# A gated scan followed by a top-1 mixture of experts: another set of planner numbers, modality numbers built by groups of runs, weights loaded between the first inputs

## The chip, the core and the metric

The kernel runs on one core of one Trainium2 chip. The metric is the device time of one execution in microseconds (us): the median of the runs, 940.31 us for the kernel before (three runs, 939.61 to 948.43). One more execution was taken with the hardware profiler; every time of a row or a stretch below is of that execution.

Engines: PE is TensorE (matmuls), DVE is VectorE, ACT is ScalarE, POOL is GpSimd, SP is SyncE. SP only issues DMAs here; its queue works in order, so a DMA whose condition is open holds up all that stand behind it. Each of the other engines works through its own instructions in order too.

## What is computed

Four sequences of 5056 tokens with 256 channels pass through a gated linear recurrence; each resulting token (20224 rows of 256) then goes through one of eight experts. Biases that depend on a token's modality (0 or 1) are added to the router's logits.

```python
a_t = np.exp(8.0 * sig_r * np.log(a_base))          # per token and channel
x_gated = np.sqrt(np.maximum(1 - a_t * a_t, 1e-6)) * sig_i * x
h = a_t[:, t] * h + x_gated[:, t]                    # for t in range(5056): y[:, t] = h
...
logits = y @ w_gate + modality_bias[modality_id]     # 8 experts
e_idx = np.argmax(logits, axis=1)
out[mask] = gate_w[mask, None] * (np.maximum(y[mask] @ w1[e], 0) @ w2[e])   # mask: e_idx == e
```

## The kernel before

**Chunks.** The scan runs over 22 chunks of time (`STEPS`: 96, three times 128, 17 times 256, 224 steps of all four sequences). A chunk's three inputs `a`, `g`, `x` are loaded by SP (`load_chunk`), ACT makes tanh, exp, square and root, DVE gates and scans (`scan_chunk`, `gate_chunk`). `size_chunk` finds a power of two that brings the chunk into 16-bit floats; `split_chunk` and `low_parts` write the result as a high part (ACT) and a low part (DVE). PE makes the logits `psl` from them (L878). `route_chunk` adds the modality bias on DVE (L950, which needs `bm` and `ivl`, both from POOL), finds the expert of each token and its slot in a table `rows` in DRAM. `rows_part` turns the split chunk into rows (four DMA transposes `rt<-a` on SP) and scatters them with indirect DMAs from POOL (L1096).

**Pages.** Two experts take most tokens (`HOT = 2`). Their tokens are worked on in pages of 128, then 256, later 512 rows: DVE chooses a page's place in `rows` (`choose_two`, the tile `sel`), SP reads that number and loads the page transposed (`X<-rows`, L1354), PE computes layer 1 (`ph`, L1452) and layer 2 (`po`, L1498). The first two pages (`Xfirst`) are not read back from DRAM: PE picks their rows out of chunk 0 (`px`, L1049). A matmul in 32-bit accuracy is made of three 16-bit ones, so every weight is split too: `convert` makes a high half (`HI`: on ACT or DVE, one letter for each of two parts) and a low half in four pieces. For a weight with `D` in `LO` DVE makes the pieces (L444); with `P` PE does, by a 32-bit matmul with a diagonal and a 16-bit one with minus the identity (`pl`, L449 and L450), and ACT copies them out (L452). Weights 0 and 1 are the two layers of the first hot expert, 2 and 3 those of the second.

**Modality numbers.** `modality_order` is one thread on POOL: it brings the modality of every token into the layout of the chunks. Chunk by chunk size it copies the numbers (`mf`, L763 and L770) and makes their complement (`mg`, L775): first chunk 0 (3 columns), then chunks 1 to 3 (12 columns), then the 17 chunks of 256 steps (136 columns), then the last chunk (7 columns). `modality_bias` then makes a chunk's `bm` on POOL (L791, L796).

**What sets the order.** The program is laid out once by a planner in the kernel: threads ask for an engine with an estimated duration; of those that could start within `WINDOW` the planner takes the one with the least rank (`place`: a base, `C_STEP` per chunk, and hand-set numbers in `RANK`). The result is a fixed order for each engine. Where the planner sees PE idle for more than 0.5 us, `fill` (L331) puts matmuls on a constant there, 1.25 times as long as the gap that it expects. A scatter waits for the page matmul that the planner had placed last before it (`count["pe"]`), so a late PE delays scatters too.

Of the kernel before, what the change touches and what calls it, by code (L numbers as in the profile page):

```python
# [46 lines left out]
WINDOW = 0.09  # L47
# [3 lines left out]
HI = ["A", "AD", "A", "AD", "A", "D"]  # L51
LO = "DDPPDD"
START = "0 1 w w w w 2"
MODALITY = 14.11
PACED = 2
AHEAD = 7.0
LAND = 1.1
SHOW = 0.5
W_AT = 11.91
C_STEP = 2.31  # L60
GROW = 1.01
SIZE_LAG = 3.0
# [3 lines left out]
SLACK = 5.0  # L66
EARLY = 4
URGENT = 0.0
ROW_STEP = 2.4
LAG = 3.0  # L70
W_RANK = [10.2, 11.1, 7.0, -6.5]
W_LOW = [3.7, 5.6, -4.4, 2.1]
PICK_AT = 6.87
PICK = 14.12
# [3 lines left out]
    "load": [0.0, 2.1, -7.6, -1.3, 0.0, 3.0, 1.1, 10.3, -1.0],  # L78
    "scan": [-1.4, -9.0, -3.3, -2.8, -0.5, -0.3, -0.9, 2.7],
    "gate": [0.0, 0.0, 0.0, 3.3, 0.0, 0.8, -1.0, -4.7, 3.7, 0.3],  # L80
    "size": [1.7, 0.0, 0.0, 0.0, 1.4, 0.0, 0.0, 0.8],
    "split": [0.0, -1.5, 0.5, -4.1, 0.0, -0.5, 0.0, 0.4, 6.0, 3.6],
    "low": [9.8, 9.6, 0.0, -12.2, 0.0, -1.7],
    "route": [-6.4, 0.0, 0.0, 0.0, 0.6, -0.3, 2.3],
    "gates": [0.0, -2.2, 4.2, 5.5, 0.0, 0.0, 0.0, 0.0, -1.0],
    "rows": [0.0, 1.1, -0.6, 0.0, 0.0, 0.0, 0.9, -3.5, 0.0, 2.2],
# [35 lines left out]
def kernel(  # L122
# [156 lines left out]
    slots = {t: Slots(n) for t, n in BUFS.items()}  # L279
    free = {"PE": 0.0, "ACT": 5.7, "DVE": 5.9, "POOL": 9.0, "DMA": 2.1, "queue": 1.2}  # L280
# [18 lines left out]
    def give(tag, n):  # L299
        slots[tag].back[n] = plan["end"]  # L300
# [261 lines left out]
    def load_chunk(c):  # L562

        t0, T = CHUNKS[c]
        cols = 2 * B * T
        base = 2 * B * t0
        z = T / 256
        got = tiles[c] = []
        if f"{c}" in loads:
            yield "SP", 0.0, seen(("turn", loads.index(f"{c}") - 1)), 0.0  # L570
        else:
            yield "SP", 0.0, allof(drained(sum(B * t for _, t in CHUNKS[: c + 1]) - BACKLOG), seen(("load", c - 1))), -3.0
        n = max(1, T // P)
        for name, src in (("a", rs), ("g", gs), ("x", xs)):
            tag = "H" if c == 0 and name != "g" else name
            for i in range(n):
                yield "DMA", 2.9 * z / n, allof(room(tag) if i == 0 else seen(), paced(c)), -9.0
                if i == 0:
                    tickets[c, name] = tag, take(tag)
                    t = (pm if tag == "H" else pa).tile([P, cols], F32, name=f"{name}{c}", tag=tag, bufs=BUFS[tag])  # L580
                    got.append(t)
                w = cols // n
                ins = LOADS.dma_start(t[:, i * w : (i + 1) * w], src[:, base + i * w : base + (i + 1) * w])
                if c >= PACED:
                    tc.add_manual_dep(
                        ins.ins, pace[-2], mybir.DependencyInfo(mybir.DependencyClass.Sync, mybir.DependencyReason.DATA)
                    )
                pace.append(ins.ins.name)
                landed.append(plan["end"] + 0.1)
            mark["load", c, name] = plan["end"] + (SLACK if c >= LATE else 0.0)  # L590
        if c == 0:
            yield "DMA", 0.2, None, -9.0
            nc.sync.dma_start(wg, w_gate.rearrange("(h p) e -> p h e", p=P))
            yield "DMA", 0.2, None, -9.0
            nc.sync.dma_start(mb, mbias.rearrange("m e -> (m e)").partition_broadcast(P))
            yield "DMA", 0.5, None, -9.0
            nc.sync.dma_start(mid, modality.bitcast(I32).rearrange("p (c two) -> p c two", two=2))
        went(f"{c}")
        mark["load", c] = plan["end"]
        if c + 1 < NC:  # L600
            start_chunk(c + 1)
# [130 lines left out]
    def modality_order():  # L732

        yield "POOL", 0.4, room("X")
        tx = take("X")
        scratch = pm.tile([P, 5, COL[-1]], BF16, name="mq", tag="X", bufs=BUFS["X"])
        first, mq = scratch[:, 4], scratch[:, 0:4]
        nc.gpsimd.tensor_copy(first, mid[:, :, 0])
        for h in range(2):
            yield "PE", 0.2, room("ph")  # L740
            tp = take("ph")
            ps = psh.tile([P, 2, 256], F32, name=f"pm{h}", tag="ph")
            for a in range(2):
                nc.tensor.matmul(
                    ps[:, a, 0 : COL[-1]], sel4[:, 2 * h + a].rearrange("p g b -> p (g b)"), first, start=True, stop=True
                )
            yield "ACT", 0.35, None
            nc.scalar.activation(mq[:, 2 * h : 2 * h + 2], ps[:, :, 0 : COL[-1]], AF.Copy)
            give("ph", tp)
        c = 0  # L750
        while c < NC:
            T, n = CHUNKS[c][1], 1
            while c + n < NC and CHUNKS[c + n][1] == T:
                n += 1
            cs = slice(COL[c], COL[c + n])
            for g in range(B):
                yield "POOL", max(1, T // P) * (0.17 + 0.022 * n) * (1 if T % P == 0 else 2), None, 0.0
                gp = slice(Q * g, Q * g + Q)
                if T % P == 0:
                    src = mq[gp, :, cs].rearrange("p a (n g w) -> p n g w a", n=n, g=B)[:, :, g]  # L760
                    to = mf[gp, cs, 0].rearrange("p (n w a) -> p n w a", n=n, a=4)
                    for w in range(T // P):
                        nc.gpsimd.tensor_copy(to[:, :, w], src[:, :, w])  # L763
                    continue
                assert n == 1
                a, A = 0, T // Q
                while a < A:
                    q = g * A + a
                    k = min(A - a, 4 - q % 4)
                    nc.gpsimd.tensor_copy(  # L770
                        mf[gp, COL[c] + a : COL[c] + a + k, 0], mq[gp, q % 4 : q % 4 + k, COL[c] + q // 4]
                    )
                    a += k
            yield "POOL", 0.15 + n * 0.01, None, 0.0
            nc.gpsimd.tensor_scalar(  # L775
                out=mg[:, cs], in0=mf[:, cs], scalar1=-1.0, scalar2=1.0, op0=ALU.mult, op1=ALU.add
            )
            for i in range(c, c + n):
                mark["modality", i] = plan["end"]
            c += n  # L780
        give("X", tx)

    def modality_bias(c):

        C = columns(c)
        yield "POOL", 0.25 + 0.125 * C, seen(("modality", c))
        shc = [P, C, E]
        mc = slice(COL[c], COL[c + 1])
        bm = sm.tile([P, C, E], F32, name=f"bm{c}", tag="bm", bufs=3)
# [10 lines left out]
    def size_chunk(c):  # L800
# [36 lines left out]
        yield "POOL", 0.2, None  # L837
        nc.gpsimd.tensor_tensor(out=ivl, in0=iv, in1=ivg, op=ALU.mult)
        mark["ivl", c] = plan["end"] + 0.2

    def split_chunk(c):
# [8 lines left out]
        add(modality_bias(c), (0, place("low", c)), plan["end"])  # L850
# [7 lines left out]
    def low_parts(c, yg, ys, sc):  # L858
# [12 lines left out]
        yield "PE", 0.35 + 0.35 * z, room("lg"), 1.25 if c > 6 else 0.0  # L871
# [16 lines left out]
    def rows_part(c, j):  # L888
# [24 lines left out]
        yield "POOL", 0.2, lambda: at, 0.0  # L913
# [3 lines left out]
        yield "POOL", 0.2, seen(("gates", c)), 0.0  # L917
# [3 lines left out]
        nc.gpsimd.tensor_scalar(  # L921
# [10 lines left out]
    def route_chunk(c):  # L932
# [19 lines left out]
        )  # L952
        yield "DVE", small, None
# [27 lines left out]
        yield "DVE", small, seen(("counted", c - 1)) if c else None  # L981
# [25 lines left out]
        yield "POOL", 0.2, None  # L1007
        bh = sm.tile([1, HOT, E], F32, name=f"bh{c}", tag="bh")
        nc.gpsimd.tensor_tensor(
# [3 lines left out]
        yield "POOL", 0.5, None, 0.0  # L1013
# [142 lines left out]

    def routed(t=FAR):
        n = 0
        while n < NC and all(mark.get(k, FAR) <= t for k in [("b2", n)] + [("put", n, j) for j in range(parts(n))]):
            n += 1  # L1160
        return n

    def enough():
# [3 lines left out]
        for c in range(NC):  # L1167
            at = max([at, mark.get(("b2", c), FAR)] + [mark.get(("put", c, j), FAR) for j in range(parts(c))])
# [7 lines left out]
    def new_page(size, e, sel, col, late):  # L1176
        pg = Page()
        pg.size, pg.st, pg.e, pg.sel, pg.col, pg.routed, pg.late = size, size, e, sel, col, routed(plan["end"]), late
        return pg
# [18 lines left out]
    def choose_two(size, full):  # L1198

        sel, ticket = new_sel()  # L1200
        b2 = tiles["b2", routed(plan["end"]) - 1 if pages else 0]
# [21 lines left out]
        for e in range(HOT):  # L1223
            pg = new_page(size, e, sel, e, not full)
# [10 lines left out]
    def choose_cold(masked):  # L1235
# [32 lines left out]
        pg = new_page(P, None, sel, 0, True)  # L1268
# [58 lines left out]
    def load_rows(n=0):  # L1327
        while True:
# [5 lines left out]
            if True:  # L1334
# [3 lines left out]
                else:  # L1338
                    yield "DMA", 0.05 + st / 140, room("X"), 0.2, 1.65 if st <= 256 else 2.9
# [46 lines left out]
    def page_gates(t):  # L1386
        pg = t.pg
        yield "POOL", 0.25, lambda: max(t.known, mark.get(("hot", pg.e), FAR) if pg.e is not None else 0.0)
# [143 lines left out]
    def start_chunk(c):  # L1532
# [4 lines left out]
        add(size_chunk(c), (0, place("size", c)), urgent=early)  # L1537
        add(split_chunk(c), (0, place("split", c)), urgent=early)
# [92 lines left out]
```

## Time and profile before

| | us |
|---|---|
| median of three runs | 940.31 |
| profiled execution, whole | 936.71 |
| its span, first to last instruction | 935.0 |
| PE busy in the span | 920.6 (98%) |
| DVE, ACT, POOL busy | 630.4, 584.5, 509.3 |
| granted TensorE clock, mean | 1.000 of full speed |

The profiled execution is 3.60 us under the median. "Busy" counts a matmul from its start to the end of its result, and neighbours overlap; so what one matmul costs PE is read from the starts of two neighbours in the timeline, not from a row's mean duration. A wait in a row's brackets is the idle time of that engine just before it, and what ended it.

### The profile page before, as it was taken

To read this page: it belongs to the slowest core of one execution; us is meant where nothing else is said; L and a number is where in the kernel's file an instruction comes from. 1 tells how busy PE (TensorE), PEld (TensorE's weight loads), DVE (VectorE), ACT (ScalarE), POOL (GpSimd) and SP (SyncE) were. 2 spreads that over 40 slices of the span, in tenths; PEclk is the share of its full clock that TensorE was granted. 3 is DMA by queue.
4 is the path that set the end of the run, shared out by engine and by line. 5 is a ranking of instruction groups with operands and counts; after the bars stand their busy time and mean duration, and the time that the engine had idled before them with its cause. 6 is when DMAs were issued, how large, how long until landed. Compare 5 with 4: busy or idle time off the path is not lost. (4 is left out here: it accounts for less than half of the span.)

```text
span 935.0 us, 19535 instructions
## 1 busy us (share of the span) xinstructions
PE 920.6 (98%) x7222; PEld 657.9 (70%) x7222; DVE 630.4 (67%) x1434; ACT 584.5 (63%) x810; POOL 509.3 (54%) x731
## 2 busy tenths in 40 slices
PE   8999999999999999999999999999999999999997
PEld 4568777888887666666666666666666666666796
DVE  7998987887989777658777684688844233423521
ACT  8898788577768857567746766576543335333422
POOL 6766676866466556564654655566664425422222
PEclk9999999999999999999999999999999999999999
DMA  9779996898899677698398677586462335313110
GB/s 316 203 204 239 274 222 194 171 258 194 217 288 193 152 212 158 130 250 200 118 180 219 217 181 203 160 188 200 101 142 66 93 89 149 92 46 125 44 40 25
DMA packets 226938, 157.88 MB, mean 169 GB/s; under 512 B 195665, under 2 KB 200146, under 8 KB 226834
## 3 DMA queue, kind: packets, MB, share of 16 engines
q1 hardware_dynamic: 210562, 112.57, 51.6%
q0 software_dynamic: 16128, 43.98, 13.6%
q8 instruction: 58, 0.95, 0.4%
q14 instruction: 46, 0.38, 0.1%
q10 hardware_dynamic: 144, 0.00, 0.0%
HBM read 70.86 MB, written 44.48 MB: 123 GB/s over the span
## 5 line engine op out<-in xcount | busy, mean ns | idle before, releaser
L1452 PE MATMUL ph<-X,hw 128*128 128x512 f16 (+1 forms) x2400 | 452.8, 332 | 5.1 <-DMA X<-rows 5.1
L1452 PEld LDWEIGHTS <-hw 128*128 128x128 f16 x2496 | 237.0, 98 | 132.1 <-DMA X<-rows 6.8
L1498 PE MATMUL po<-hw,H 128*128 128x256 f16 x2448 | 298.4, 273 | 0.7 <-DVE H L1382 0.6
L1410 POOL DMA_INDIRECT out_dram<-ot,mt x160 | 182.0, 1137 | 183.0 <-ACT ot L1399 136.2
L1498 PEld LDWEIGHTS <-H 128*128 128x128 f16 x2496 | 241.9, 98 | 53.6 <-issue 1.6
L1096 POOL DMA_INDIRECT rows<-rt,di x158 | 181.4, 1148 | 170.4 <-PE ph L1452 79.4
L1382 DVE SCALAR_TENSOR_TENSOR H<-ph,H 128x512 f16<-128x512 f32 (+1 forms) x216 | 141.9, 665 | 130.0 <-ACT H L1380 129.3
L1380 ACT ACTIVATE H<-ph 128x512 f16<-128x512 f32 (+1 forms) x216 | 123.1, 578 | 134.3 <-PE ph L1452 128.4
L1498 PE MATMUL po<-hw,Hb 128*128 128x256 f16 x1344 | 165.1, 273 | 0.0
L1498 PEld LDWEIGHTS <-Hb 128*128 128x128 f16 x1344 | 130.6, 98 | 36.7 <-issue 0.8
L1382 DVE SCALAR_TENSOR_TENSOR Hb<-ph,Hb 128x512 f16<-128x512 f32 x112 | 76.6, 686 | 100.3 <-ACT Hb L1380 100.0
L1399 ACT ACTIVATE ot<-po,gt 128x256 f32<-128x256 f32 x160 | 75.4, 472 | 91.1 <-PE po L1498 78.2
L1380 ACT ACTIVATE Hb<-ph 128x512 f16<-128x512 f32 x112 | 66.4, 594 | 99.8 <-PE ph L1452 99.2
L669 DVE TENSOR_TENSOR_SCAN g<-a,g 128x512 f32<-128x512 f32 (+2 forms) x77 | 94.2, 1240 | 0.6
L652 DVE SCALAR_TENSOR_TENSOR g<-x,g 128x1024 f32<-128x1024 f32 (+2 forms) x39 | 48.1, 1233 | 24.4 <-ACT x L647 24.4
L865 DVE SCALAR_TENSOR_TENSOR a<-g,scy,a 128x512 f16<-128x512 f32 (+3 forms) x88 | 58.5, 695 | 4.9 <-ACT a L853 4.8
L853 ACT ACTIVATE a<-g,scy 128x512 f16<-128x512 f32 (+3 forms) x88 | 55.6, 672 | 2.7 <-DVE scy L700 2.0
L641 ACT ACTIVATE a<-a,ch 128x1024 f32<-128x1024 f32 (+3 forms) x44 | 49.6, 1148 | 0.0
L626 DVE SCALAR_TENSOR_TENSOR g<-g,x 128x1024 f32<-128x1024 f32 (+2 forms) x39 | 48.2, 1238 | 0.0
L807 DVE TENSOR_REDUCE top<-x 128x4 f32<-128x2048 f32 (+3 forms) x22 | 45.2, 2056 | 4.1 <-DMA x<-in_x_dram 4.1
L331 PE MATMUL fill<-onesb 128*128 128x512 bf16 x182 | 44.9, 396 | 1.1 <-DVE onesb L152 1.1
L647 ACT ACTIVATE x<-x,quarter 128x2048 f32<-128x2048 f32 (+3 forms) x22 | 40.2, 1828 | 0.3
(216 smaller groups left out, 675.5 us busy)
## 6 DMA issues: line engine op xcount, KB each, us to landing
a<-in_r_gate_dram SPq DMA_DIRECT2D x37, 512.0 KB
g<-in_i_gate_dram SPq DMA_DIRECT2D x37, 512.0 KB
x<-in_x_dram SPq DMA_DIRECT2D x37, 512.0 KB
wr<-in_moe_w_dram SPq DMA_DIRECT2D x4, 1024.0 KB
cw<-in_moe_w_dram SPq DMA_DIRECT2D x4, 1024.0 KB
out_dram<-ot,mt POOLq DMA_INDIRECT x160
rows<-rt,di POOLq DMA_INDIRECT x158
rt<-a SPq DMA_TRANSPOSE x88
```

Of the source, the lines that this page charges most:

```text
L626: nc.vector.scalar_tensor_tensor(out=g, in0=g, scalar=1.0, in1=x, op0=ALU.add, op1=ALU.mult)
L641: nc.scalar.activation(sl, sl, AF.Exp, scale=ch[:, h : h + 1], bias=ch[:, h : h + 1])
L669: nc.vector.tensor_tensor_scan(out=gi, data0=ai, data1=gi, initial=0.0, op0=ALU.mult, op1=ALU.add)
L853: nc.scalar.activation(ys[:, 0, :, g], yg[:, :, g, :].rearrange("p h (k b) -> p h k b", b=Q), AF.Copy, scale=sc[:, g : g + 1])
L865: nc.vector.scalar_tensor_tensor(out=ys[:, 1, :, g], in0=yg[:, :, g, :].rearrange("p h (k b) -> p h k b", b=Q), scalar=sc[:, g : g + 1], i ...
L1096: ins = nc.gpsimd.indirect_dma_start(out=rows[:, :], out_offset=bass.IndirectOffsetOnAxis(ap=idx, axis=0), in_=src, in_offset=None, bounds ...
L1380: nc.scalar.activation(hi, src, AF.Relu)
L1382: nc.vector.scalar_tensor_tensor(out=lo, in0=src, scalar=0.0, in1=hi, op0=ALU.max, op1=ALU.subtract)
L1399: nc.scalar.activation(t.ot[a // 2][:, a % 2, :], po, AF.Copy, scale=t.gt[:, a : a + 1])
L1410: ins = nc.gpsimd.indirect_dma_start(out=out[:, :], out_offset=bass.IndirectOffsetOnAxis(ap=t.mt[:, a, 0:1], axis=0), in_=t.ot[a // 2][:, ...
L1452: ins = nc.tensor.matmul(to, wv[:, s, k, f * P : (f + 1) * P], cur.X[:, 2 * x + k, :], start=(m == 0), stop=(m == len(mm) - 1))
L1498: ins = nc.tensor.matmul(po, H[:, hx, fi, a * P : (a + 1) * P], wv[:, wx, f], start=(f == 0 and m == 0), stop=(f == NF - 1 and m == 2))
```

## The change

The diff leaves what is computed as it is. Its core, without the estimates that only the planner reads (durations in `yield` lines):

```diff
-START = "0 1 w w w w 2"
+START = "0 w 1 w w 2 w"
-LO = "DDPPDD"
+LO = "PDPPDD"
-HI = ["A", "AD", "A", "AD", "A", "D"]
+HI = ["A", "AD", "DA", "A", "A", "D"]
-AHEAD = 7.0
+AHEAD = 6.41
+AHEAD_OF_ROWS = 1.04
+ON_DVE = 8
+BIAS_RANK = 3.19
-    "load": [0.0, 2.1, -7.6, -1.3, 0.0, 3.0, 1.1, 10.3, -1.0],
+    "load": [0.0, 0.0, -0.9, -2.8, -0.1, 0.0, 0.0, 0.0, 3.1],
...
-        c = 0
+        left, c = [NC], 0
         while c < NC:
...
-            for i in range(c, c + n):
-                mark["modality", i] = plan["end"]
+            add(modality_part(c, n, mq, left, tx), (0, 9 if c == 0 else min(place("load", c), MODALITY_LAST) - 0.5), plan["end"])
             c += n
...
-        yield "POOL", 0.2, None
-        nc.gpsimd.tensor_tensor(out=ivl, in0=iv, in1=ivg, op=ALU.mult)
+        yield "DVE" if c < ON_DVE else "POOL", 0.1 if c < ON_DVE else 0.35, None
+        (nc.vector if c < ON_DVE else nc.gpsimd).tensor_tensor(out=ivl, in0=iv, in1=ivg, op=ALU.mult)
...
-        add(modality_bias(c), (0, place("low", c)), plan["end"])
+        if c >= ON_DVE:
+            add(modality_bias(c), (0, place("low", c)), plan["end"])
...
-        nc.gpsimd.tensor_scalar(
+        (nc.vector if c < ON_DVE else nc.gpsimd).tensor_scalar(
             out=rt.bitcast(F32)[:, 0:k, D + 1], in0=sg[:, cs], scalar1=ivf, scalar2=None, op0=ALU.mult
...
+        if c < ON_DVE:
+            b2 = tiles["b2", c] = sm.tile([1, HOT], F32, name=f"b{c}", tag="b2", bufs=8)
+            for r in range(HOT):
+                yield "DVE", 0.1, None, 0.0 if r else None
+                nc.vector.scalar_tensor_tensor(
+                    out=bh[:, r], in0=be[0:1], scalar=1.0, in1=hm[:, r], op0=ALU.mult, op1=ALU.mult, accum_out=b2[:, r : r + 1]
+                )
+            mark["held", c] = mark["b2", c] = plan["end"] + 0.2
+            return
...
-                    yield "DMA", 0.05 + st / 140, room("X"), 0.2, 1.65 if st <= 256 else 2.9
+                    yield "DMA", 0.05 + st / 140, allof(room("X"), lambda: pg.landed), 0.2, 1.65 if st <= 256 else 2.9
...
+        if c < ON_DVE:
+            add(modality_bias(c), (0, place("load", c) + BIAS_RANK))
```

So: `modality_order` hands each group of equal chunks to a thread of its own (`modality_part`), which can stand behind other POOL work; the bias of the first eight chunks is asked for from the chunk's start on; for these chunks six small POOL instructions (`ivl`, the gates' product into `rt`, the sums `b`) become four on DVE; weight 0 is loaded ahead of chunk 1 and weight 3 behind chunk 2; the low half of weight 0 is made by PE instead of DVE; a page may be chosen before its last rows have landed, and its load then waits for them; all ranks differ.

The new order on POOL, just behind the constants (`mf`, `mg`: modality numbers; `bm`, `bn`: a chunk's bias, 24 columns for chunk 0, 32 for chunk 1). Before:

```order
L738 CAST mq<-mid 128x158
...
L763 COPY mf<-mq 32x12 x4
L775 TENSOR_SCALAR mg<-mf 128x12
L763 COPY mf<-mq 32x17x4 x8
L775 TENSOR_SCALAR mg<-mf 128x136
L770 COPY mf<-mq 32x4
...
L775 TENSOR_SCALAR mg<-mf 128x7
L914 TENSOR_SCALAR rt_0_524<-tid 128x3
L838 TENSOR_TENSOR ivl_530<-ivy_468,ivg 128x1
L791 TENSOR_TENSOR bm_697<-mf,mb 128x24
L791 TENSOR_TENSOR bn_698<-mg,mb 128x24
```

After, at the same place:

```order
L744 CAST mq<-mid 128x158
...
L775 COPY mf<-mq 32x12 x4
L788 TENSOR_SCALAR mg<-mf 128x12
L804 TENSOR_TENSOR bm_527<-mf,mb 128x24
L804 TENSOR_TENSOR bn_528<-mg,mb 128x24
L809 TENSOR_TENSOR bm_527<-bm_527,bn_528 128x24
L775 COPY mf<-mq 32x17x4 x8
L788 TENSOR_SCALAR mg<-mf 128x136
L928 TENSOR_SCALAR rt_0_509<-tid 128x3
```

The bias of chunk 0 has moved ahead of the eight copies of the 17 large chunks and of the ten small copies of the last one; the latter now stand between the scatters of chunk 0.

On SP, from the first expert weight (`wr`) on; `a`, `g`, `x` of 1024 columns are the inputs of chunks 1, 2 and 3, `rt` is the transpose of a chunk's rows. Before (the three rows that read a weight's number are left out):

```order
L484 DMA wr_269<-in_moe_w_dram 128x2x1024
...
L484 DMA wr_380<-in_moe_w_dram 128x8x256
L583 DMA a_444<-in_r_gate_dram 128x1024
L583 DMA g_464<-in_i_gate_dram 128x1024
L906 DMA_TRANSPOSE rt_0_524<-a_250 128x3x128 x4
L583 DMA x_645<-in_x_dram 128x1024
L906 DMA_TRANSPOSE rt_0_702<-a_259 128x4x128 x2
```

After:

```order
L490 DMA wr_263<-in_moe_w_dram 128x2x1024
L589 DMA a_279<-in_r_gate_dram 128x1024
L589 DMA g_283<-in_i_gate_dram 128x1024
L589 DMA x_285<-in_x_dram 128x1024
...
L920 DMA_TRANSPOSE rt_0_509<-a_250 128x3x128
L589 DMA x_614<-in_x_dram 128x1024
...
L490 DMA wr_623<-in_moe_w_dram 128x8x256
L589 DMA a_672<-in_r_gate_dram 128x1024
```

Weight 0 (`wr_263`) now stands ahead of chunk 1's inputs, and weight 3 (`wr_623`) behind the transposes of chunk 0 and the `x` of chunk 2.

On PE, the stretch that ends with the first matmul of an expert (`Xfirst`); `pt` is a weight's scale, `px` the picking of the first pages. Before:

```order
L977 MATMUL psl_544<-oh_783,um_157 128x24
...
L331 MATMUL fill_814<-onesb 128x512
...
L878 MATMUL psl_821<-a_259,wg_234 32x128
...
L331 MATMUL fill_866<-onesb 128x512
...
L1049 MATMUL px_876<-pick_846,rt_0_524 128x256
...
L1452 MATMUL ph_0_923<-Xfirst,hw_0_228 128x128
```

After:

```order
L992 MATMUL psl_573<-oh_659,um_157 128x24
...
L337 MATMUL fill_723<-onesb 128x512
...
L407 MATMUL pt_739<-wr_623 128x128
...
L1073 MATMUL px_763<-pick_701,rt_0_509 128x256
...
L1481 MATMUL ph_0_831<-Xfirst,hw_0_228 128x128
```

The scale of weight 3 (`pt_739`), which stood ahead of this stretch before, now stands between chunk 0's routing and the picking of the first pages. In the whole program PE has 147 `fill` matmuls instead of 182, and 12 pairs of `pl` instead of 8. Ahead of the first `Xfirst` row stand 88 fills (before 124); between it and the first page that is read back from DRAM 32 (before 23), and 8 `pl` pairs (before 4), while the layer 2 of the second page, 24 matmuls, has moved behind that row; later among the pages 6, 18 and 3 fills (before 14 and 21). All its other matmuls are the same in number and shape, and the 53 layer-1 pages up to the program's end follow each other in the same sizes and for the same experts.

## Rows read from the trace of the kernel before

**Rows 1.** Busy time of PE in stretches of the span: the stretch, its length, PE busy and instructions, granted clock, DMA share and GB/s.

```profile
60.00:100.00 40.00, 37.93 (x350) 1.00 0.92 222
100.00:200.00 100.00, 96.12 (x877) 1.00 0.86 213
200.00:400.00 200.00, 200.00 (x1660) 1.00 0.81 197
900.00:935.00 35.00, 29.29 (x292) 0.99 0.07 24
```

**Rows 2.** The five longest waits of PE in the span: who waited for what, us in total, times, the longest.

```profile
PE ph L1452 <- DMA X<-rows: 5.1, 5, 1.8
PE fill L331 <- DVE onesb L152: 1.1, 1, 1.1
PE po L1498 <- DVE H L1382: 0.6, 1, 0.6
PE pt L401 <- DMA wr<-in_moe_w_dram: 0.6, 1, 0.6
PE psg L680 <- DVE mxg L718: 0.5, 1, 0.5
```

**Rows 3.** Timeline of PE, selected rows in order of time: start, us, line, operation, count, and the wait ahead of it.

```profile
11.04 0.22 PE L680 MATMUL psz<-identb,mxy 128*4 128x128 bf16 x1
...
16.59 1.09 PE L401 MATMUL pt<-wr 128*128 128x128 bf16 x16 [0.55 <-DMA wr<-in_moe_w_dram]
...
29.31 4.48 PE L331 MATMUL fill<-onesb 128*128 128x512 bf16 x20
33.63 0.28 PE L414 MATMUL pt<-ss,onesf 128*128 128x1 f32 x2
...
34.84 1.02 PE L449 MATMUL pl<-wr,dg 128*128 128x512 f32 x2
35.70 0.38 PE L450 MATMUL pl<-hw,nid 128*128 128x512 f16 x1
35.92 1.02 PE L449 MATMUL pl<-wr,dg 128*128 128x512 f32 x2
...
45.84 1.50 PE L1452 MATMUL ph<-Xfirst,hw 128*128 128x128 f16 x24
...
52.95 2.78 PE L1498 MATMUL po<-hw,H 128*128 128x256 f16 x24
55.67 0.41 PE L878 MATMUL psl<-a,wg 128*32 128x128 f16 x16
...
69.12 2.79 PE L1452 MATMUL ph<-X,hw 128*128 128x256 f16 x24 [1.84 <-DMA X<-rows]
...
145.84 5.41 PE L1452 MATMUL ph<-X,hw 128*128 128x256 f16 x48 [1.45 <-DMA X<-rows]
```

**Rows 4.** Timeline of POOL around the bias of chunk 0.

```profile
22.85 4.04 POOL L763 COPY mf<-mq 32x68 bf16<-32x68 bf16 x8
...
32.69 0.42 POOL L775 TENSOR_SCALAR mg<-mf 128x7 bf16<-128x7 bf16 x1
...
34.13 0.23 POOL L796 TENSOR_TENSOR bm<-bm,bn 128x24 f32<-128x24 f32 x1
```

**Rows 5.** Timeline of DVE: its second instruction, the logits of chunk 0 and their bias, the bias of chunk 2, the choice of the third and fourth page, chunk 4's slots.

```profile
2.03 0.16 DVE L174 TENSOR_REDUCE top<-mb 1x2 f32<-1x16 f32 x1 [0.96 <-DMA mb<-n_moe_modality_bias_dram]
...
23.02 0.24 DVE L942 TENSOR_REDUCE l<-lt 128x24 f32<-128x48 f32 x1
...
34.47 0.24 DVE L950 SCALAR_TENSOR_TENSOR l<-l,ivl,bm 128x24 f32<-128x24 f32 x1
...
62.61 0.27 DVE L950 SCALAR_TENSOR_TENSOR l<-l,ivl,bm 128x32 f32<-128x32 f32 x1 [1.21 <-POOL ivl L838]
...
64.77 0.15 DVE L1209 SCALAR_TENSOR_TENSOR sel<-u,d 1x2 int32<-1x2 f32 x1
...
110.21 0.25 DVE L1004 TENSOR_REDUCE di<-dt 128x8 int32<-128x64 f32 x1
```

**Rows 6.** Timeline of SP: the four expert weights, the transposes of chunk 0 and of chunk 2, the first page read back.

```profile
6.53 6.80 SPq L484 DMA_DIRECT2D wr<-in_moe_w_dram  x4
...
20.64 6.29 SPq L906 DMA_TRANSPOSE rt<-a  x4
27.02 0.54 SPq L583 DMA_DIRECT2D x<-in_x_dram  x1
...
56.34 5.21 SPq L906 DMA_TRANSPOSE rt<-a  x4
65.71 1.27 SPq L1354 DMA_TRANSPOSE X<-rows  x1
```

**Rows 7.** Groups of POOL instructions from 0 to 130 us: line, operation, count, busy us, mean ns of one, idle time before them and what ended it; then two of one group from the timeline.

```profile
L1017 POOL TENSOR_TENSOR bh<-bh 1x8 f32<-1x8 f32 (+1 forms) x10 | 5.3, 534 | 0.6
...
L921 POOL TENSOR_SCALAR rt<-sg,ivy 128x4 f32<-128x4 f32 (+2 forms) x5 | 3.3, 668 | 13.0 <-DVE lm L816 8.0 <-DVE sg L1089 5.0
...
L838 POOL TENSOR_TENSOR ivl<-ivy,ivg 128x1 f32<-128x1 f32 x5 | 3.1, 621 | 5.4 <-DVE mxy L821 4.6 <-DVE ivy L705 0.7
...
62.37 0.20 POOL L838 TENSOR_TENSOR ivl<-ivy,ivg 128x1 f32<-128x1 f32 x1
63.26 1.27 POOL L838 TENSOR_TENSOR ivl<-ivy,ivg 128x1 f32<-128x1 f32 x1 [0.69 <-DVE ivy L705]
```

## What the change should do to the time

> **What bounds the kernel now.** I first read the stretches of PE, since PE is busy for 98% of the span. From 200 us on it does not pause until the tail; what it leaves idle lies before 200 us and in the last 35 us [rows 1]. So the time is PE's own program plus its pauses in the first fifth. Which pauses these are the list of waits says: page rows that come back from DRAM late (5.1 us in five waits), one weight (0.6) and one layer-2 matmul that waits for DVE (0.6); 1.1 and 0.5 us belong to the launch, ahead of anything the change moves [rows 2]. The timeline of PE adds what the waits hide: its early time is spent on fills. Twenty of them take from 29.31 to 33.63, 0.216 us each; all 182 take 39 us [rows 3]. A fill is not a wait: PE must go through it even if the next real matmul is ready. So PE can gain in three ways only: fewer fills, less other work, shorter waits.
>
> The other engines then show what the fills were put there for. Chunk 0's logits are on DVE at 23.26 us, but their bias is added at 34.47, just after POOL ends that bias at 34.36 [rows 4, 5]. POOL was at the modality numbers of the large chunks and of the last chunk from 22.85 to 33.11 [rows 4]. The first expert matmul is at 45.84, the first page read back at 69.12 [rows 3].
>
> **The change, part by part.**
>
> *Fills.* 35 fewer at 0.216 us: -7.6 us. This is certain as work, since the order is fixed.
>
> *Weight 0's low half on PE.* Four more `pl` pairs. One takes 0.86 us (34.84 to 35.70) and 0.22 (to 35.92), 1.08 together [rows 3]: +4.3 us. On DVE four pieces of the same weight go. On ACT four copies come; what they delay there is the second expert's halves, and the 29 fills (6.3 us) that now stand on PE ahead of the last of these cover it; without that cover the copies would be PE's.
>
> *Modality numbers behind the first bias.* The 10.3 us of POOL from 22.85 to 33.11 now follow chunk 0's bias, so POOL can deliver it some ten microseconds earlier. By itself that shortens nothing on PE; it is what makes the smaller number of fills possible. Ahead of `Xfirst` 36 fills fall away, 7.8 us, so by its own program PE is there at 38.1 instead of 45.84. The last chunk's ten copies now sit between chunk 0's scatters; at the old end of that group (33.11) nothing needs them, and chunk 0's rows are read back only for numbers of the first pages: I cost that at nothing, and if the cover went it would be their 5 us on POOL, bounded by the slack of page 3.
>
> *Six POOL instructions per chunk become four on DVE, for eight chunks.* POOL's groups cost 0.53 us (`bh`, two per chunk), 0.67 and 0.62 us each [rows 7]: 2.4 us per chunk from the groups shown. On DVE a comparable small instruction is 0.15 us (the choice at 64.77) [rows 5], so 0.6 us per chunk. Both lie beside PE's work; what counts is the hand-overs: the bias of chunk 2 waited 1.21 us on DVE for POOL's `ivl` [rows 5], and the gates' product on POOL had 13.0 us of idle ahead of it [rows 7]. These two hand-overs go for chunks 0 to 7.
>
> One row of `ivl` took 0.20 us and the next one 1.27 us, with the same shape [rows 7]. The Trainium skill ("SBUF — State Buffer", Who interferes with whom) says that a DVE instruction with two SBUF inputs and a POOL one that reads SBUF exclude each other for a whole instruction. By that rule the moved instructions would have cost POOL only 0.2 us each without DVE's traffic, and the copies of the modality numbers, now beside the routing, may hold DVE up in turn. The two durations fit the rule, and no row here shows a DVE instruction held up so; the sum would not change, since neither engine's busy time is in it.
>
> *Weights between inputs.* Weight 0 now precedes chunk 1. PE meets its scale right after the first 29 fills, where before `psz` stood at 11.04 [rows 3]. Four weights were issued from 6.53 to 13.33 [rows 6] and the first was used at 16.59 after a wait of 0.55, with chunk 1's 1.5 MB ahead of it [rows 2, 3]. Of the 2.5 MB up to its end 1.5 no longer go first, so of its 10.1 us between 0 and six tenths fall away: it is there between 10.6 and 16.59, and PE waits between 0 and 5.6 us. I take 12.5 us, a wait of 1.5, nearer to the early end because the inputs are the larger share. Weight 3 now stands behind chunk 0's transposes and `x`, which ended at 27.56 [rows 6]; PE needs it at about 34.5 (38.1 less picking, five fills and its scale). The first weight took 10.1 us from issue to use (6.53 to 16.59) with four loads underway: upper bound 37.6, a wait of 3.1; lower bound below nothing, none. I take none, because one load stands ahead of it instead of three.
>
> *The first page read back.* PE's program up to it: 27 fills fewer net (-5.8), four pairs more (+4.3), 24 layer-2 matmuls moved behind it (52.95 to 55.67: -2.7), the longer wait for weight 0 (+0.9): without its own wait PE arrives at 69.12 - 1.84 - 3.3 = 64.0. Are the rows there? The choice stood at 64.77; adding up DVE's rows in each order with this trace's durations, 57.2 us of work (182 rows) stood ahead of it and 52.0 us (168 rows) do now, first row 2.03; with the 1.21 us wait for `ivl` gone it comes at 58.4. But SP's four transposes of chunk 2 stand ahead of that load and ended at 61.55; from issue (65.71) to PE (69.12) it took 3.4 us [rows 5, 6]. If the transposes stay where they were, PE gets the page at 65.8; if they move with DVE, at 62.7. I take 65.0: a wait of 1.0, bounds 0 and 1.8.
>
> *Later pages.* Of before, 3.2 us of waits for rows and 0.6 for DVE remain behind that page. Chunk 3's gates and their product no longer hold its scatters back, but chunk 4's slots (110.21 before) have 98.8 us of DVE work ahead of them instead of 95.8 [rows 5]. Bounds: 0, and as much as keeps page 9 (145.84) where it was. I take 1.0, near the lower end, because fills (6 and 18) still stand ahead of two of these pages.
>
> *Sum.* Fills -7.6, pairs +4.3, waits from 6.3 to 1.5 + 1.0 + 1.0 = 3.5, so -2.8: together **-6.1 us**. Against the profiled execution's own 936.71 that is 930.6. The median lies 3.60 above that execution, so 934.2 for the median. Nothing is added behind 200 us: PE does the same 53 pages there, back to back, so what it gains early it keeps.
>
> **Rivals.**
>
> *All waits vanish.* If rows, weights and `H` are always there, -7.6 + 4.3 - 6.3 = -9.6: 930.7 for the median. For it speaks the routing that starts ten microseconds earlier; against it SP, whose transposes still stand ahead of the page loads.
>
> *Nothing arrives.* Page 9's rows depend on chunk 4, whose slots moved back by 3.0 us in DVE's order. If that page starts at 145.84 as before, PE fills the gap with waiting, and only the three fills behind it count: +0.6, 941.0. For it speaks that order, and that scatters wait for PE; against it that DVE's waits ahead of it, for POOL and for a late PE, shrink.
>
> *Slower: weight 3 stops PE.* Its scale stands in PE's program ahead of the picking of the first pages, so a late weight holds everything. From 34.5 us on each microsecond of its landing is one of the total; at 40.6, 13 us after its issue, the gain of 6.1 is used up, and past that the kernel is slower: 944 if it lands at 44, over 1% if at 50. Against it: the first weight took 10.1 us with more ahead of it [rows 3, 6].
>
> *The clock falls.* PE's granted clock is 1.00 in every stretch but the tail [rows 1], and waits of up to 1.84 us did not lower it [rows 2]. A longer pause in the place of fills might; at half the clock 24 matmuls of 256 columns would take 2.7 us more. The Trainium skill ("TensorE: Matmul & The Clock Gate", Part 1) says that the clock follows PE's recent activity and falls when it idles; no wait that I expect is longer than those of before, so I leave it at 2 in 100, inside the slower case.
>
> **How the numbers follow.** My forecast, between -3 and -9 us: 0.55. All waits gone, or nearly (-9 to -10): 0.17. Nothing arrives (-3 to +2): 0.20. Slower by more, weight 3 or the clock: 0.08. The time is that of the likeliest, 934.2. The range takes in both neighbours: from 930 (the floor of 930.7 and some spread of a median) to 942 (941.0 and the same), which leaves out the slower case and half of a case at the floor. The likeliest alone spans 931.2 to 937.2. About 1%, 9.4 us, is what a measurement of this kernel can tell from no change; below 930.9 lies only the floor case's better part, 0.13; above 949.7 the slower case's worse part, 0.05; the rest, 0.82, is within 1%.
>
> **What would show it.** `Xfirst` near 38 us and the first page read back near 65; one wait of one to two microseconds for weight 0 and none at weight 3's scale; DVE's bias of chunk 0 directly behind its logits; page 9 near 139 (145.84 less the sum, and less the three fills behind it). PE without a pause from some 180 us to the tail, and a tail as before. Wrong would be a wait for `wr` of several microseconds near 34, or more row waits than 5.1 us in all.

## The result, and the profile after

| | before | after |
|---|---|---|
| median of seven runs | 941.45 us | 947.61 us |
| profiled execution, its span | 936.71, 935.0 | 947.61, 945.9 |
| PE busy, the rest of the span | 920.6, 14.4 | 918.5, 27.4 |

The changed kernel takes 1.006 times as long, 95% interval 1.0038 to 1.0083: slower by about 6 us, within the 1% either way that was called no change. The forecast was 934.2 us and a range of 930 to 942. PE's own work shrank by 2.1 us (forecast: 3.3), but it stood idle for 13.0 us more.

The stretches of PE, as in [rows 1], with one stretch added, from 40 to 60 us:

```profile
40.00:60.00 20.00, 9.90 (x65) 0.74 0.56 126
60.00:100.00 40.00, 37.21 (x329) 1.00 0.80 205
100.00:200.00 100.00, 97.75 (x917) 1.00 0.95 234
200.00:400.00 200.00, 197.77 (x1660) 1.00 0.82 198
```

Before, the added stretch read:

```profile
40.00:60.00 20.00, 19.72 (x207) 1.00 0.84 239
```

The loss has one place: half of the 20 us from 40 on, where the granted clock falls too. A small second one lies behind 200 us, where PE had no pause before. The list of PE's waits, as in [rows 2], names them:

```profile
PE psz L697 <- DVE dmy L693: 10.1, 1, 10.1
PE ph L1481 <- DMA X<-rows: 3.5, 3, 2.2
PE ph L1481 <- DVE sg L1113: 1.9, 1, 1.9
PE pt L407 <- DMA wr<-in_moe_w_dram: 1.5, 1, 1.5
PE fill L337 <- DVE H L1411: 1.5, 1, 1.5
```

The timeline of PE, as in [rows 3]:

```profile
11.49 1.09 PE L407 MATMUL pt<-wr 128*128 128x128 bf16 x16
...
35.62 1.09 PE L407 MATMUL pt<-wr 128*128 128x128 bf16 x16 [1.50 <-DMA wr<-in_moe_w_dram]
...
39.52 0.83 PE L1481 MATMUL ph<-Xfirst,hw 128*128 128x128 f16 x12
...
53.84 0.16 PE L697 MATMUL psz<-dmy,onesb 4*128 4x4 bf16 x1 [10.10 <-DVE dmy L693]
...
53.96 2.08 PE L455 MATMUL pl<-wr,dg 128*128 128x512 f32 x2
55.83 0.63 PE L456 MATMUL pl<-hw,nid 128*128 128x512 f16 x1
...
77.73 1.47 PE L1481 MATMUL ph<-X,hw 128*128 128x256 f16 x12
...
154.72 1.48 PE L1481 MATMUL ph<-X,hw 128*128 128x256 f16 x12 [0.81 <-DMA X<-rows]
...
344.56 1.46 PE L1481 MATMUL ph<-X,hw 128*128 128x512 f16 x6 [2.23 <-DMA X<-rows]
```

Until 43 us the kernel goes much as was forecast: the first expert matmul stands at 39.52 instead of 45.84. Then PE waits 10.1 us for a tiny DVE instruction (`dmy`, the scale of a chunk). What had DVE been waiting for? Its timeline, at chunk 1's bias:

```profile
53.39 0.28 DVE L964 SCALAR_TENSOR_TENSOR l<-l,ivl,bm 128x32 f32<-128x32 f32 x1 [10.82 <-POOL bm L809]
53.58 0.21 DVE L693 TENSOR_SCALAR dmy<-identx,m1y 4x5 bf16<-4x5 f32 x1
```

`dmy` itself was ready; it stands behind the bias of chunk 1 in DVE's order, and that waits for POOL. POOL's timeline, where [rows 4] showed all copies done at 33.11:

```profile
31.21 1.39 POOL L783 COPY mf<-mq 32x4 bf16<-32x4 bf16 x7
33.67 2.04 POOL L1120 DMA_INDIRECT rows<-rt,di  x1 [1.08 <-issue]
43.30 0.18 POOL L783 COPY mf<-mq 32x1 bf16<-32x1 bf16 x1 [7.58 <-DMA rows<-rt,di]
44.04 0.98 POOL L1120 DMA_INDIRECT rows<-rt,di  x1 [0.55 <-POOL mf L783]
48.31 0.19 POOL L783 COPY mf<-mq 32x3 bf16<-32x3 bf16 x1 [3.29 <-DMA rows<-rt,di]
49.05 0.98 POOL L1120 DMA_INDIRECT rows<-rt,di  x1 [0.55 <-POOL mf L783]
52.13 0.19 POOL L783 COPY mf<-mq 32x4 bf16<-32x4 bf16 x1 [2.09 <-DMA rows<-rt,di]
```

Of the last chunk's ten copies, which the part on the change puts between the scatters, seven stand ahead of the first scatter (31.21); each of the last three stands behind one scatter. Each of these three takes 0.2 us, but waits until the scatter ahead of it has landed: 7.58, 3.29 and 2.09 us, 13.0 together. The next scatter stands behind the copy, so the three transfers follow each other where they could overlap. The built program shows the waits as conditions on semaphores, those of POOL's DMAs in brackets; so they are part of the program:

```
95 L783 COPY mf<-mq 32x1 [waits DMASW2_49]
96 L1120 DMA rows<-rt_0_509,di_695 164352x258 [waits Pool_49]
97 L783 COPY mf<-mq 32x3 [waits DMASW3_49]
98 L1120 DMA rows<-rt_0_509,di_695 164352x258 [waits Pool_49]
99 L783 COPY mf<-mq 32x4 [waits DMASW4_49]
```

A scatter's row is short, 2.04 us, and hides this: the landing that the copy waits for came 7.6 us behind the row's end (33.67 + 2.04 to 43.30). The Trainium skill ("Perfetto Trace Analysis", DMA Instruction — SWDGE (GPSIMD)) says that the profiler ends such a row when the descriptors are written, not when the data has moved; the trace agrees, with these 7.6 us.

### The profile page after: what moved, and what is told of

Same layout as the page of the kernel before. It is cut to its first block, busy times and chain, and to the rows that moved or that the text cites. A ratio compares the mean times of both kernels' runs of the same rounds, so it can differ in the third digit from the quotient of the medians.

```text
span 945.9 us, 19483 instructions
## 1 busy us (share of the span) xinstructions
PE 918.5 (97%) x7199; PEld 657.0 (69%) x7199; DVE 633.6 (67%) x1478; ACT 587.1 (62%) x815; POOL 478.4 (51%) x683
## 5 line engine op out<-in xcount | busy, mean ns | idle before, releaser
L1439 POOL DMA_INDIRECT out_dram<-ot,mt x160 | 172.4, 1078 | 235.2 <-ACT ot L1428 167.4
L1120 POOL DMA_INDIRECT rows<-rt,di x158 | 177.8, 1125 | 172.6 <-PE po L1527 68.7
L651 ACT ACTIVATE x<-a 128x2048 f32<-128x2048 f32 (+3 forms) x22 | 38.1, 1732 | 16.3 <-DVE g L632 15.6
```

The costliest lines, as they stand in the source:

```text
L1120: ins = nc.gpsimd.indirect_dma_start(out=rows[:, :], out_offset=bass.IndirectOffsetOnAxis(ap=idx, axis=0), in_=src, in_offset=None, bounds ...
L1439: ins = nc.gpsimd.indirect_dma_start(out=out[:, :], out_offset=bass.IndirectOffsetOnAxis(ap=t.mt[:, a, 0:1], axis=0), in_=t.ot[a // 2][:, ...
```

## The experiments

Each is compared with the kernel before on the same chip, as a ratio with its 95% interval. Their lines lie up to 21 further down than in the changed kernel. The first four move only the POOL instructions named; every other engine's order is the changed kernel's. Only the second and the last of the eight times lie in a range given beforehand; the others lie up to 1.9 us outside the nearest one. A gain by the ratios and the same gain by the medians differ by up to 2 us here.

**Ten copies ahead of the scatters.** `pieces` lists the last chunk's ten copies; the planner's steps stay, and all ten are issued in the first.

```diff
                 yield "POOL", 0.36 if c == 0 else 0.5, None, 0.0
-                nc.gpsimd.tensor_copy(
...
+                here = [(g, a, q, k)] if c == 0 else pieces if (g, a) == (0, 0) else []
+                for gg, aa, qq, kk in here:
...
+                    nc.gpsimd.tensor_copy(
```

> The changed kernel, with the ten small copies of the last chunk's modality numbers together ahead of the first scatter of chunk 0; every other instruction of every engine keeps its place. Theory (landing): three of those copies, which stand between and behind the scatters, each wait until the scatter ahead of them has landed (13.0 us on POOL), and the bias of chunk 1 behind them holds DVE for 10.8 us and with it PE for 10.1. Then here the three scatters go out within about 4 us of each other, the bias of chunk 1 is there near 39 us, DVE and PE don't stop at 43, the clock stays at full speed, and of 947.6 us some 12 fall away (10.1 of wait, about 1.9 of matmuls at half the clock): 935 to 937. Rival one (queue): POOL can't issue the second scatter before the first has moved its data, copies or not; then the bias still comes near 50 and the time stays within 2 us of 947.6. Rival two (next wait): the stop at 43 goes, but weights or transposes that were hidden behind it stop PE for most of it a few us later; then 942 to 946.

938.87 us, 0.9979 (0.9965 to 0.9993). POOL's timeline:

```profile
30.68 1.94 POOL L794 COPY mf<-mq 32x4 bf16<-32x4 bf16 x10
33.43 2.04 POOL L1131 DMA_INDIRECT rows<-rt,di  x1 [0.81 <-POOL mf L794]
35.77 0.97 POOL L1131 DMA_INDIRECT rows<-rt,di  x1 [0.30 <-issue]
37.04 0.97 POOL L1131 DMA_INDIRECT rows<-rt,di  x1 [0.30 <-issue]
...
38.78 0.25 POOL L820 TENSOR_TENSOR bm<-bm,bn 128x32 f32<-128x32 f32 x1
```

Between one scatter's row and the next lie 0.3 us, the bias of chunk 1 is there at 39.03 instead of 53.36, and PE does not stop. That falsifies the queue rival: POOL issues a scatter while earlier ones move. Of the 12 us expected, 8.7 came by the medians, 7.6 by the ratios (1.006 less 0.9979, of 941). About 1 us of the rest is a page near 335 us, for which PE waits 3.25 us where it waited 2.23 in the changed kernel (at 344.56 there). Another part shows in one row and what follows it: weight 3 was later than in the changed kernel, and the first picking behind its scale took 1.48 us where there it took 0.82.

```profile
36.53 1.44 PE L407 MATMUL pt<-wr 128*128 128x128 bf16 x16 [2.59 <-DMA wr<-in_moe_w_dram]
37.77 1.48 PE L1084 MATMUL px<-pick,rt 128*128 128x256 f16 x6
```

**Ten copies behind the scatters.** The same edit, with all ten issued in the last step.

> The changed kernel, with the ten small copies together behind the three scatters of chunk 0, still ahead of the bias of chunk 1. Theory (landing): one wait in the place of three; the scatters go out back to back by about 38 us and overlap, the wait ends some 7.6 us behind (the first landing took that after its issue), near 45, the copies take 2 to 4 us, the bias is there near 49, PE stops for about 5 to 6 us instead of 10.1: 941 to 943. Rival (queue): as in the changed kernel, within 2 us of 947.6.

941.36 us, 1.002 (1.0001 to 1.004): the time is the one expected, but by luck, since PE's stop is 1.0 us where 5 to 6 were expected. POOL has one wait in the place of three, and the first two copies, to partitions 0 to 31, had gone ahead without it:

```profile
43.85 1.60 POOL L794 COPY mf<-mq 32x1 bf16<-32x1 bf16 x8 [5.19 <-DMA rows<-rt,di]
```

The bias comes at 46.48, DVE waits 1.7 us for it and PE 1.0. The profiled executions of this kernel and the first lie 0.9 us apart (939.50 and 938.62), as that stop would have it; the medians lie 2.5 apart, and what makes the rest is not shown.

**Bias of chunk 1 early.** The copies stay between the scatters.

```diff
+        if c != 1:
+            bias_now(c)
+        if c == 0:
+            bias_now(1)
```

> The changed kernel, with the bias of chunk 1 made directly behind that of chunk 0; the copies stay between the scatters, and POOL waits there as before. Theory (landing, and the bias behind it): POOL still waits some 13 us for the three scatters, but nothing that DVE needs then stands behind them before chunk 2's bias; DVE and PE don't stop at 43, and the time is that of the kernel with the copies ahead, 935 to 938. Rival (the late scatters themselves): the rows of chunk 0 or POOL's later work are what is late; then PE stops behind 43 us for page rows instead, and the time is 942 or more.

940.77 us, 1.0019 (0.9999 to 1.0039). POOL still waits 11.2 us for the scatters, and neither DVE nor PE stops at 43: the wait costs nothing where nothing needed stands behind it. But the time lies between the theory's range and the rival's: 1.9 us by the medians, 3.8 by the ratios, of what the first experiment gained is missing. The rival's stop for page rows near 43 us is not there. The three lists of waits, of SP, DVE and PE, show another road from the late scatters:

```profile
SPq L1392 <- DMA rows<-rt,di: 4.8, 1, 4.8
...
DVE top L828 <- DMA x<-in_x_dram: 4.0, 1, 4.0
...
PE psz L686 <- DVE mxy L842: 2.5, 1, 2.5
```

SP's load of a first page's row numbers waits for the last scatter; chunk 4's inputs stand behind it in SP's queue, DVE waits for its `x`, and PE for DVE, at 64.31. No run takes this road alone, so how much of the loss it makes is not shown.

**Other copies between the scatters.** The two that write partitions 0 to 31 stand there, the eight that write partitions 32 and up ahead.

```diff
+                here = [(g, a, q, k)] if c == 0 else {0: pieces[2:], 7: pieces[0:1], 8: pieces[1:2]}.get(pieces.index((g, a, q, k)), [])
```

> The changed kernel again with copies between the scatters of chunk 0, but other ones: the two that write partitions 0 to 31 stand between the scatters, the eight that write partitions 32 and up stand ahead of the first. In the program only copies of the second kind carry a wait for the landing of the scatters ahead of them. Theory (landing): no copy waits now, POOL's scatters go out within some 5 us, the bias of chunk 1 is there near 40 us, no stop at 43; the time is that of the kernel with all ten copies ahead, 0.998 of before (938 to 940). Rival (any POOL work between two scatters waits for the first): a stop of several us as in the changed kernel, 943 to 948.

937.65 us, 0.9975 (0.9955 to 0.9994). POOL:

```profile
33.77 2.04 POOL L1131 DMA_INDIRECT rows<-rt,di  x1 [1.08 <-issue]
35.86 0.18 POOL L794 COPY mf<-mq 32x4 bf16<-32x4 bf16 x1
36.20 0.98 POOL L1131 DMA_INDIRECT rows<-rt,di  x1 [0.16 <-issue]
```

So it is not work between two scatters that costs, it is the wait that a copy carries; and only copies from partition 32 on carry it.

**Weight 3 early** (on top of the first experiment): its load is issued on SP behind the `g` of chunk 2.

```diff
+            if c == 2 and name == "g":
+                tiles["wr", 3] = raw_weight(3)
```

> The changed kernel with the ten copies ahead of the scatters (the kernel of the first run here, 938.9 us), and the load of weight 3 issued on SP ahead of the transposes of chunk 0 instead of behind them and the x of chunk 2; every other instruction keeps its place. Theory (weight 3 late): PE waited 2.6 us for that weight at its scale, and behind that wait the matmuls up to the first expert matmul took 5.44 us where the changed kernel's, after a wait of 1.5, took 3.90; both go: 938.9 less 4.1, 934.5 to 935.5, first expert matmul near 38. Rival (the bytes): the load is as large as an input of a chunk and takes the queues from the x of chunk 2, and from the transposes; what PE gains at the weight it waits for later at the scales and the logits of chunks 1 and 2: 937 or more.

936.27 us, 0.9954 (0.9935 to 0.9974). The wait for the weight is gone and the first expert matmul is at 37.83. By the ratios 2.4 us came of the 4.1 (0.9979 less 0.9954, of 941). The list of PE's waits shows where the rest went:

```profile
PE psz L694 <- DVE mxy L853: 3.0, 1, 3.0
```

This is DVE behind the `x` of chunk 4 again (4.2 us on DVE). PE came earlier only to wait for an input.

**A page's load ahead of transposes** (on top of the first experiment): in the planner, chunk 11's transposes wait until the page with the index 24 has been issued.

```diff
+        page = seen(("loaded", 24)) if c == 11 else None
```

> The kernel of the first run here (938.9 us), with the load of one 512-row page on SP ahead of three transposes of chunk 11 that it stood behind; nothing else moves. Theory (queue): those transposes wait for a scatter to free their buffer (16.5 us on SP, until 321.5), the page's load behind them starts at 327.4 and PE waits 3.25 us for it at 335.6; issued at once the page is there before PE: 935 to 936, and PE has no pause from 200 us to the tail. Rival (rows or choice): the page is chosen or its rows land only then; no change, 938 to 940.

934.64 us, 0.9938 (0.9917 to 0.9958). PE has 200.00 us of 200 between 200 and 400 us, and by the ratios 3.9 us came where 3.25 were expected (0.9979 less 0.9938, of 941). SP's timeline, with the load ahead:

```profile
318.64 2.09 SPq L1395 DMA_TRANSPOSE X<-rows  x1
320.93 0.42 SPq L1396 DMA_DIRECT2D mt<-rows  x1
321.68 6.94 SPq L932 DMA_TRANSPOSE rt<-a  x4
```

**Both together.**

> Both together: weight 3 issued early and the page's load ahead of chunk 11's transposes. If the two theories hold, the savings of 4.1 and 3.25 add up, since they lie 300 us apart on PE's own program: 931 to 932, faster than the kernel before by 8 us (0.9%). If an earlier PE only meets the next late row, a good part is given back: 934 to 937.

933.97 us, 0.9929 (0.9909 to 0.9949): 7.0 us under the median of the kernel before on that chip, and the fastest version here. Early weight and early page do not add up: over the page alone the weight brings 0.9 us by the ratios, within their intervals. The longest waits of PE are now all of 2 us or less:

```profile
PE fill L337 <- DVE H L1432: 2.0, 1, 2.0
PE psg L694 <- DVE mxg L732: 2.0, 1, 2.0
PE ph L1502 <- DMA X<-rows: 1.5, 2, 1.3
```

**Twenty fills less**, on top of both.

```diff
-            for _ in range(max(1, int(n))):
+            for _ in range(9 if int(n) == 29 else max(1, int(n))):
```

> The kernel with both changes (934.0 us), with 20 of the 29 fills that PE runs from 47.9 us on left out; nothing else moves. Reading one (a fill is PE's own program, as the forecast counted it): 20 times 0.216, 4.3 us less: 929.5 to 930. Reading two (PE only fills a wait for the inputs of chunk 4): DVE waits 2.2 us for the x of chunk 4 near 58 and PE 1.2 us for DVE at 61.4, so a PE that comes earlier waits longer, there and for H behind it; the time stays within 1 us of 934.0, with some 4 us more of waits between 48 and 70.

933.97 us, 0.9935 (0.9911 to 0.9959): no difference. A new wait stands in the place of the fills, with slower matmuls behind it, and at the next point where PE waits for DVE it is there at the same time as with them (61.17 and 61.39):

```profile
53.24 0.38 PE L456 MATMUL pl<-hw,nid 128*128 128x512 f16 x1 [2.56 <-ACT hw L467]
53.46 1.45 PE L455 MATMUL pl<-wr,dg 128*128 128x512 f32 x2
...
61.17 0.22 PE L694 MATMUL psz<-identb,mxy 128*4 128x128 bf16 x1 [1.17 <-DVE mxy L853]
```

## Why the prediction was wrong

**The step that failed** is the one on the modality numbers: "The last chunk's ten copies now sit between chunk 0's scatters; ... I cost that at nothing, and if the cover went it would be their 5 us on POOL". Only three of the ten stand behind a scatter, but these three are the loss. The prediction asked who needs the copies' results (nobody), and took the copies' own duration for the bound. It did not ask what the copies wait for, nor what stands behind them. They wait 13.0 us for landings; the bias of chunk 1 stands behind them; DVE, in order, needs it at 42.6 and holds `dmy` behind it. The first and the fourth experiment remove the wait and, by the ratios, 7.6 and 8.0 us of the time, and the third shows that the wait alone stops nobody at 43 when that bias is ahead of it.

**The clock** was given 2 in 100, on waits of up to 1.84 us that had not lowered it. Behind the wait of 10.1 us two `pl` matmuls took 2.08 us where a pair takes 1.02, so they ran at 1.2 in place of 2.4 GHz: the granted clock from 53.8 to 56.2 us is 0.50. It is a consequence of the stop: from 53.96 to 57.67 PE took 3.71 us for two `pl` pairs that take 1.08 each before, some 1.6 us more. The length of a wait alone did not decide it. The clock also fell behind waits of 2.06 to 2.59 us for weight 3 in three experiments, and not behind one of 1.50. But at one page it stayed at 1.00 behind a wait of 3.25 us in the first experiment, and fell to 0.51 behind one of 2.20 in the fourth, with the same six matmuls behind both:

```profile
335.57 1.46 PE L1492 MATMUL ph<-X,hw 128*128 128x512 f16 x6 [3.25 <-DMA X<-rows]
333.69 2.72 PE L1492 MATMUL ph<-X,hw 128*128 128x512 f16 x6 [2.20 <-DMA X<-rows]
```

**The waits** were to shrink from 6.3 to 3.5 us. Behind the launch they are about 19.6 us in the changed kernel. Apart from the stop, its terms were off too: weight 0 is there in time (11.49, forecast 1.5 us late); weight 3, forecast in time, is 1.5 us late, inside its bounds of 0 and 3.1; "nothing is added behind 200 us" is wrong by 2.2, a page's load behind transposes that wait for a buffer, shown by the experiment that puts it ahead.

**Fills and pairs**, -7.6 and +4.3, are right as counts: with the stops mended PE's busy time is 4.9 us under that of before (915.7), where 3.3 was forecast. But "PE must go through it even if the next real matmul is ready" was argued from PE alone. The last experiment takes 4.3 us of fills away and nothing changes: there PE fills a wait for converted weights and inputs. Fewer fills are a gain only where what follows them comes earlier too. How much of the 7.6 is such a gain stays open.

**The sum.** With the copies, weight 3 and the page moved, the kernel is 7.0 us faster than before by the medians, 6.7 by the ratio, near the forecast of 6.1. That is in part luck and no proof of the terms: weights, waits and fills came out otherwise one by one. Adding 3.60 us to the profiled execution for the median was not wrong for the kernel before: of its 61 runs beside the experiments 59 lie above 936.71. It doesn't carry over: the changed kernel's profiled execution is its median. Why that execution of before was so short stays open.

**The marks** that were named: the first expert matmul came at 39.52 (forecast near 38, which leaves out the 0.9 us more for weight 0 that its own sum has; 37.98 with the stops mended), the first page read back at 77.73 (65; 66.37), page 9 at 154.72 (139; 143.23). The front of the forecast holds where nothing stops PE; page 9 is late by 4 us there too, since waits for DVE stand ahead of it and it waits 1.27 us for its own rows.

**The rivals.** "Nothing arrives" had a late page for its cause, "weight 3 stops PE" a late weight. The weight was late by 1.5 us, not by 13. Neither looked at POOL. What would show it wrong was named as a weight wait near 34 or row waits beyond 5.1 us; both stayed small (1.5 and 3.5), and the loss came through a third door.

## What to carry to other kernels

When an instruction moves into another place of an in-order queue, cost three things: its own time, what it waits for there, and who waits for what now stands behind it. Small work between indirect DMAs is the case to look at in the built program: if it carries a wait for their landing, the DMAs no longer overlap and everything behind them in that queue is late. Filler work in front of a wait is not a cost until the thing waited for comes earlier.

## What the runs showed of the hardware

The three landings in a row ended 7.6, 3.3 and 2.1 us behind their scatters' rows. During the first, the transposes of a chunk and the load of an input were under way (SP's rows from 33.17 to 39.56 us); weight 3 was there already. In the second experiment, with 0.3 us between the rows, the three cost one wait that ended 5.5 us behind the last row.

Only copies from partition 32 on carry such a wait: the order of the built program says so, and the second and fourth experiments bear it out. Why the program is built like that was not tried. The Trainium skill ("GPSIMD Engine Reference", 2.1 Instruction dispatch) says that consecutive POOL instructions are no barrier between its cores, which serve 16 partitions each, and that a reader of what another core wrote then needs a wait on the producer's completion. These copies read nothing that a scatter wrote, so that alone would not ask for the wait, and its reason stays open.
